# Moving every sixth softmax exponential of a two-layer transformer kernel from ScalarE to VectorE

## The chip, the cores and the metric

One core of one Trainium2 chip (trn2). The metric is the device time of one execution in microseconds (us). The kernel before takes 2283 us; most of its executions lie within 0.3% of each other. Engines are named as in the profile: PE is TensorE's matmuls, PEld its weight loads, ACT ScalarE, DVE VectorE, POOL GpSimd.

## The reference

Two layers, each an attention block and a feed-forward block with a residual, on 2048 rows of 512:

```python
def _A_ref(x, wqkv, wo):                      # S = 2048, D = 512
    H = 32; Dh = D // H                       # 32 heads of only 16
    qkv = transpose((x @ wqkv).reshape(B, S, 3, H, Dh), 2, 0, 3, 1, 4)
    scores = einsum("bhqd,bhkd->bhqk", q, k) * Dh ** -0.5
    p = softmax(scores)
    o = einsum("bhqk,bhkd->bhqd", p, v)
    return o.transpose(...).reshape(B, S, D) @ wo

def _B_ref(x, w1, w2):                        # F = 1792
    return silu(x @ w1) @ w2

x = x + _A_ref(layernorm(x), wqkv, wo)        # layer 0
x = x + _B_ref(layernorm(x), w1, w2)
x = x + _A_ref(layernorm(x), wqkv, wo)        # layer 1, the same weights
x = x + _B_ref(layernorm(x), w1, w2)
```

With heads of 16 the exponentials are many and the matmuls thin: 2 x 32 x 2048 x 2048 exponentials, in 4096 blocks of 128 keys by 512 queries.

## The kernel before

A "block" is one 128 x 512 piece of scores of one head. 64 blocks (16 key tiles of 4 heads) make a "group", whose result is one PSUM bank `o_ps` (a tile of 128 x 512 in fp32 is called a bank here). Blocks are taken three at a time. A step computes three scores, issues the P.V matmuls of the tile two steps back, and gives one exponential over 1536 columns to ACT:

```python
tiles = [blocks[i : i + NB] for i in range(0, len(blocks), NB)]      # NB = 3
...
for t, blks in enumerate(tiles):
    ...                                     # bg.ensure(...) of K, Q, V where needed
    s_ps = ps_s.tile([P, NB, 512], FP32, name="s_ps", tag="s")       # bufs=2: 6 PSUM banks
    for i, (L, qc, g, par, kt, j) in enumerate(blks):
        r = slice(32 * j, 32 * j + 32)
        nc.tensor.matmul(                   # scores: 32 rows of the array, 128 columns
            s_ps[:, i, :],
            lhsT=KT[L, kt // 4][r, g, (kt % 4) * P : (kt % 4 + 1) * P],
            rhs=QT[L, qc][r, g, par, :], start=True, stop=True)
    if t >= 2:
        emit_pv(t - 2)
    p_tiles[t] = ppool.tile([P, NB, 512], BF16, name="p_sb", tag="p")
    nc.scalar.activation(p_tiles[t][...], s_ps[...], ACT.Exp, scale=float(SCALE))
    if urgent:
        run_urgent()                        # transposes of a finished group
    else:
        bg.pump()                           # one piece of background work

def emit_pv(tile_i):
    for i, (L, qc, g, par, kt, j) in enumerate(tiles[tile_i]):
        ...
        nc.tensor.matmul(                   # P.V: 128 rows, 32 columns
            o_ps[32 * j : 32 * j + 32, :],
            lhsT=VA[L, kt // 4][:, kt % 4, 17 * h : 17 * h + 32],
            rhs=p_sb[:, i, :], start=(kt == 0), stop=(kt == NKT - 1))
        if kt == NKT - 1 and j == 3:        # group complete
            nc.vector.tensor_copy(out=oT[:], in_=o_ps[:])
            urgent.append(...)
```

All else (layer norms, Q, K, V and output projections, the feed-forward block) is "background": generators that `bg.pump()` advances by one piece a step. They share one PSUM bank (`ps_m`). Of the eight banks that the program uses six hold scores, one `o_ps`, one the background. The three score matmuls of a step use different 32-row strips of the array and run side by side (three within 0.61 us in the timeline below); so do the P.V matmuls in different 32-column strips.

The softmax here doesn't subtract the row's maximum and nothing guards it: scores larger than these inputs give would overflow.

## Time and profile before

| | before |
|---|---|
| time | 2283.2 us (median of 13) |
| exp on ACT | 1366 instructions, 1868 us busy |
| DVE busy | 414 us, 18% |
| PE busy | 1855 us, 81% |
| mean granted TensorE clock | 0.72 of full speed |

From the page of the kernel before. Busy time of the engines, then two of the rows that cut the span into 40 slices, in tenths (ACT busy, granted TensorE clock):

```profile
PE 1855.4 (81%) x10240; PEld 538.3 (24%) x10240; DVE 414.4 (18%) x746; ACT 1914.6 (84%) x1479; POOL 36.4 (2%) x47
...
ACT  1499989999999989999506999899989899999941
...
PEclk9995558985799767985666555799567965788556
```

ACT is full except at the start, at the layer boundary (slices 20 to 22) and in the tail. The clock is far from full in many slices.

The three costliest groups of the page (line, engine, operation, output<-inputs, shapes, count | busy us, mean ns of one | idle before them and its releaser):

```profile
L467 ACT ACTIVATE p_sb<-s_ps 128x1536 bf16<-128x1536 f32 x1366 | 1868.0, 1536 | 240.5 <-PE s_ps L456 239.5
L456 PE MATMUL s_ps<-QT,KT 32*128 32x512 bf16 x4096 | 705.3, 504 | 183.3 <-ACT p_sb L467 165.4
L399 PE MATMUL o_ps<-p_sb,VA 128*32 128x512 bf16 x4096 | 731.4, 513 | 42.0 <-DVE oT L408 41.8
```

A stretch of plain attention, no background work, in the windows view of the kernel before (busy us of each engine and number of instructions, then clock):

```profile
core 0: us, PE busy (x) PEld busy (x) DVE busy (x) ACT busy (x) POOL busy (x), PEclk, DMA share, GB/s
228.00:285.00 57.00, 48.90 (x257) 12.86 (x254) 2.75 (x6) 55.34 (x42) 0.00 (x0) 0.50 0.00 1
```

42 exponentials in 57 us, ACT 97% busy, and the clock exactly half. The timeline of the kernel before there (start, length, what):

```profile
227.56 6.98 ACT L467 ACTIVATE p_sb<-s_ps 128x1536 bf16<-128x1536 f32 x5
...
229.22 0.61 PE L456 MATMUL s_ps<-QT,KT 32*128 32x512 bf16 x3 [0.19 <-ACT p_sb L467]
...
229.77 0.61 PE L399 MATMUL o_ps<-p_sb,VA 128*32 128x512 bf16 x3
...
230.56 0.61 PE L456 MATMUL s_ps<-QT,KT 32*128 32x512 bf16 x3 [0.18 <-ACT p_sb L467]
```

One step takes 1.34 us. PE's two passes follow each other at 0.54 us and 0.80 us, of which 0.19 us is waiting for ACT: at half clock PE is nearly full too. In the same trace background matmuls of 512 columns, all of one shape, start 0.43 us apart at half clock and 0.23 at full (medians), so about 0.1 us of each 0.54 us comes on top. A pass of three matmuls side by side costs about 0.1 us more than one such background matmul at either clock (0.54 us against 0.43 at half, 0.32 against 0.23 at full); why, no run tested.

### The profile page before, as it was taken

How to read it: one execution, taken by the hardware profiler on the slowest of the kernel's cores; microseconds unless marked ns; L12 is line 12 of the kernel's file. 1: busy time of each engine (PE TensorE's matmuls, PEld its weight loads, DVE VectorE, ACT ScalarE, POOL GpSimd, SP SyncE). 2: the span in 40 equal slices, each digit the busy share in tenths (PEclk: the TensorE clock that was granted, in tenths of full speed). 3: DMA queues.
4: the chain of work that ended last, by engine and by line, in shares of the span. 5: the costliest groups of instructions: out<-in, count | busy, mean ns of one | idle time of the engine just before them, and what ended most of it. 6: DMA issues, size and time to landing. Idle time of an engine off the chain costs nothing.

```text
span 2282.7 us, 24321 instructions
## 1 busy us (share of the span) xinstructions
PE 1855.4 (81%) x10240; PEld 538.3 (24%) x10240; DVE 414.4 (18%) x746; ACT 1914.6 (84%) x1479; POOL 36.4 (2%) x47
## 2 busy tenths in 40 slices
PE   5788888888878888888667888878888888888866
PEld 1222222222222222222222222222222222222222
DVE  4430012120312112120221000311012100210021
ACT  1499989999999989999506999899989899999941
POOL 1100000000000000000000000000000000000000
PEclk9995558985799767985666555799567965788556
DMA  4000000000000000000000000000000000000000
GB/s 138 0 1 1 1 1 1 1 1 1 1 1 1 1 1 1 1 1 1 1 0 1 1 1 1 1 1 10 1 1 1 6 5 1 1 1 10 1 0 9
DMA packets 7917, 11.51 MB, mean 5 GB/s; under 512 B 384, under 2 KB 6784, under 8 KB 7808
## 3 DMA queue, kind: packets, MB, share of 16 engines
q1 hardware_dynamic: 7808, 9.96, 1.3%
q8 instruction: 80, 1.31, 0.2%
q14 instruction: 29, 0.24, 0.0%
HBM read 7.86 MB, written 2.10 MB: 4 GB/s over the span
## 4 chain that ended last, share of the span: by engine, by line
ACT 42%; PE 26%; issue 23%; DVE 9%; POOL 0%; DMA 0%; ACTq 0%; POOLq 0%; DVEq 0%
ACT p_sb L467 39%; PE s_ps L456 6%; PE o_ps L399 5%; PE h_ps L310 4%; ACT t_sb L320 3%; PE q_ps L214 2%; DVE QT L224 2%; PE f_ps L334 2%; PE v_ps L235 2%; PE k_ps L197 2%; DVE oT L408 2%; PE t_ps L177 1%; PE att L253 1%; DVE hT L321 1%; DVE st L152 1%
## 5 line engine op out<-in xcount | busy, mean ns | idle before, releaser
L467 ACT ACTIVATE p_sb<-s_ps 128x1536 bf16<-128x1536 f32 x1366 | 1868.0, 1536 | 240.5 <-PE s_ps L456 239.5
L456 PE MATMUL s_ps<-QT,KT 32*128 32x512 bf16 x4096 | 705.3, 504 | 183.3 <-ACT p_sb L467 165.4
L399 PE MATMUL o_ps<-p_sb,VA 128*32 128x512 bf16 x4096 | 731.4, 513 | 42.0 <-DVE oT L408 41.8
L456 PEld LDWEIGHTS <-KT 32*128 32x128 bf16 x4096 | 223.2, 95 | 726.5 <-issue 708.9
L399 PEld LDWEIGHTS <-VA 128*32 128x32 bf16 x4096 | 144.7, 98 | 500.2 <-issue 500.2
L310 PE MATMUL h_ps<-fT,w_sb 128*128 128x512 bf16 x448 | 169.1, 481 | 64.0 <-DVE hT L321 61.8
L408 DVE CAST oT<-o_ps 128x512 bf16<-128x512 f32 x64 | 44.1, 689 | 755.2 <-PE o_ps L399 754.8
L320 ACT ACTIVATE t_sb<-h_ps 128x512 f32<-128x512 f32 x112 | 73.5, 657 | 105.9 <-PE h_ps L310 105.9
L321 DVE SCALAR_TENSOR_TENSOR hT<-t_sb,h_ps 128x512 bf16<-128x512 f32 x112 | 77.0, 688 | 389.5 <-ACT t_sb L320 389.5
L334 PE MATMUL f_ps<-w_sb,hT 128*128 128x512 bf16 x448 | 129.5, 394 | 10.8 <-DVE hT L321 5.0
L310 PEld LDWEIGHTS <-w_sb 128*128 128x128 bf16 x448 | 39.4, 109 | 146.2 <-issue 142.2
L224 DVE TENSOR_SCALAR QT<-q_ps,mask 128x512 bf16<-128x512 f32 x64 | 45.1, 746 | 144.1 <-PE q_ps L214 144.1
L177 PE MATMUL t_ps<-ident,xn 128*128 128x128 bf16 x256 | 36.2, 308 | 38.6 <-DVE xn L163 33.1
L235 PE MATMUL v_ps<-w_qkv,xnT 128*128 128x512 bf16 x128 | 51.7, 531 | 18.5 <-DVE VA L244 12.7
L343 DVE SCALAR_TENSOR_TENSOR x_sb<-f_ps,x_sb 128x512 bf16<-128x512 f32 x32 | 22.1, 692 | 216.6 <-PE f_ps L334 216.6
L214 PE MATMUL q_ps<-xnT,w_qkv 128*128 128x512 bf16 x128 | 49.4, 478 | 14.1 <-DVE QT L224 13.1
L253 PE MATMUL att<-ident,oT 128*128 128x128 bf16 x256 | 35.0, 283 | 31.3 <-DVE hT L321 12.0
L197 PE MATMUL k_ps<-xnT,w_qkv 128*128 128x512 bf16 x128 | 47.1, 470 | 10.2 <-DVE xnT L182 3.9
L334 PEld LDWEIGHTS <-hT 128*128 128x128 bf16 x448 | 32.7, 99 | 67.9 <-issue 52.4
L289 PE MATMUL y_ps<-wo_sb,aT 128*128 128x512 bf16 x128 | 43.0, 428 | 4.6 <-DVE aT L283 1.6
L152 DVE BATCH_NORM_STATS2 st<-x_sb 128x6 f32<-128x512 bf16 x64 | 42.7, 667 | 3.0 <-DMA x_sb<-in_A_x_dram 3.0
L253 PEld LDWEIGHTS <-oT 128*128 128x128 bf16 x256 | 21.0, 121 | 88.8 <-issue 65.9
(30 smaller groups left out, 320.1 us busy)
## 6 DMA issues: line engine op xcount, KB each, us to landing
w_sb<-in_B_w_dram SPq DMA_DIRECT2D x2, 1792.0 KB, 14.1
x_sb<-in_A_x_dram SPq DMA_DIRECT2D x4, 512.0 KB, 8.8
out_dram<-x_sb SPq DMA_DIRECT2D x16, 128.0 KB, 1.7
w_qkv<-in_A_wqkv_dram SPq DMA_DIRECT2D x1, 1536.0 KB, 7.3
wo_sb<-in_A_wo_dram SPq DMA_DIRECT2D x1, 512.0 KB, 9.5
```

What stands on the lines that cost most here:

```text
L197: nc.tensor.matmul(k_ps[:], lhsT=w_qkv[:, ct, D + P * g : D + P * (g + 1)], rhs=xnT[L, c][:, ct, :], start=(ct == 0), stop=(ct == CT - 1),)
L214: nc.tensor.matmul(q_ps[:], lhsT=w_qkv[:, ct, P * g : P * (g + 1)], rhs=xnT[L, c][:, ct, :], start=(ct == 0), stop=(ct == CT - 1),)
L224: nc.vector.tensor_scalar_mul(out=QT[L, c][:, g, par, :], in0=q_ps[:], scalar1=masks[par][:, 0:1])
L235: nc.tensor.matmul(v_ps[:], lhsT=xnT[L, c][:, ct, tq * P : (tq + 1) * P], rhs=w_qkv[:, ct, 2 * D : 3 * D], start=(ct == 0), stop=(ct == CT ...
L310: nc.tensor.matmul(h_ps[:], lhsT=w1_sb[:, ct, ft * P : (ft + 1) * P], rhs=fT[:, ct, :], start=(ct == 0), stop=(ct == CT - 1),)
L320: nc.scalar.activation(t_sb[:], h_ps[:], ACT.Tanh, scale=0.5)
L321: nc.vector.scalar_tensor_tensor(out=hT[:, ft, :], in0=t_sb[:], scalar=1.0, in1=h_ps[:], op0=ALU.add, op1=ALU.mult,)
L334: nc.tensor.matmul(y_ps[:], lhsT=hT[:, ft, tq * P : (tq + 1) * P], rhs=w2_sb[:, ft, :], start=(ft == 0), stop=(ft == FT - 1),)
L399: nc.tensor.matmul(o_ps[32 * j : 32 * j + 32, :], lhsT=VA[L, kt // 4][:, kt % 4, 17 * h : 17 * h + 32], rhs=p_sb[:, i, :], start=(kt == 0) ...
L408: nc.vector.tensor_copy(out=oT[:], in_=o_ps[:])
L456: nc.tensor.matmul(s_ps[:, i, :], lhsT=KT[L, kt // 4][r, g, (kt % 4) * P : (kt % 4 + 1) * P], rhs=QT[L, qc][r, g, par, :], start=True, sto ...
L467: nc.scalar.activation(p_tiles[t][:, 0:n, :].rearrange("p a b -> p (a b)"), s_ps[:, 0:n, :].rearrange("p a b -> p (a b)"), ACT.Exp, scale= ...
```

## The change

The intent is to relieve ACT. ACT's tiles become 3 and 2 blocks in turn. At a rate of 0.6 a step one further block goes to DVE, which builds the exponential from bit operations: it scales the score into the bits of an fp16 number `y` whose exponent field is the integer part of the power of two, splits off the exponent (`e`) and the mantissa (`r`), and makes `r` into a cubic correction, so that exp = e + r up to a common factor. The sum `e + r` is not formed on DVE; both are multiplied by V, two P.V matmuls accumulating into the same `o_ps` strip. Besides, the transposes of a finished group are issued one step later (`due`), and the Q projections are spread, one group ahead, instead of in lumps.

```diff
-    NB = 3
+    D_RATE = 0.6
+    D_LAST = 52
-    ps_s = ...(name="ps_s", bufs=2, ...)
+    ps_s = ...(name="ps_s", bufs=1, ...)          # tags s3, s2, sd: 3 + 2 + 1 banks
@@ blocks into steps
+    while pos < len(blocks):
+        n = 3 - len(steps) % 2
+        a = blocks[pos : pos + n]; pos += n
+        d = []
+        credit = min(credit + D_RATE, 1.5)
+        if credit >= 1.0 and pos < len(blocks) and pos % 64 < D_LAST:
+            d = blocks[pos : pos + 1]; pos += 1; credit -= 1.0
+        steps.append((a, d))
@@ the exponential on DVE (emit_d, step_d; up to two blocks at a time)
+        nc.vector.tensor_scalar(out=pr["y"][:, len(pr["blks"]), :], in0=s_ps[:],
+            scalar1=float(1024 * SCALE * math.log2(math.e)),
+            scalar2=float(1024 * (15 - SHIFT)), op0=ALU.mult, op1=ALU.add)      # PSUM -> uint16
+            nc.vector.tensor_scalar(out=rf.bitcast(I32), in0=y.bitcast(I32),
+                scalar1=0x03FF03FF, scalar2=0x3C003C00, op0=ALU.bitwise_and, op1=ALU.bitwise_or)
+            nc.vector.tensor_scalar(out=ef.bitcast(I32), in0=y.bitcast(I32),
+                scalar1=0x7C007C00, scalar2=None, op0=ALU.bitwise_and)
+                nc.vector.tensor_tensor(out=rf, in0=rf, in1=rf, op=ALU.mult)
+                nc.vector.tensor_scalar(out=rf, in0=rf, scalar1=EXP_C, scalar2=EXP_A,
+                                        op0=ALU.mult, op1=ALU.add)
+                nc.vector.tensor_tensor(out=rf, in0=rf, in1=y.bitcast(FP16), op=ALU.mult)
@@ two P.V matmuls for each such block
+        for i, blk in enumerate(pr["blks"]):
+            pv(blk, [pr["e"][:, i, :].bitcast(FP16), pr["r"][:, i, :].bitcast(FP16)])
@@ main loop
+            due = bool(urgent)
...
-            if urgent:
+            if due:
                 run_urgent()
```

(Not shown: the pool sizes that make room, the bookkeeping of pairs and stages, and `next_q`, which queues one Q projection as each pair of groups begins.)

## The prediction

> **What bounds the kernel now.** In steady attention, the exponential on ACT: the page has ACT 84% busy, 1868 us in 1366 exp ACTIVATEs; the timeline at 228-236 us shows a three-block tile each 1.34 us; the windows view has ACT busy 55.3 of 57 us there. PE is close behind: the clock row reads 0.5 wherever no projection or FFN matmul runs, and a tile's score and P·V passes then take 0.54 us each, 1.08 of 1.34 us. At full clock they take 0.325 each. A pair of 128x512 background matmuls adds 0.54 us (full) or 0.97 (half). Of the 1366 tiles 733 have no background matmul, 599 of those at half clock. About 250 us at start, layer boundary (1110-1220 us) and tail are not limited by exp.
>
> **What the change does.** ACT tiles become alternately 3 and 2 blocks, still 1366 steps; 681 blocks (17%) get their exponential on DVE. ACT: 1.34 + about 0.91 us for two steps, 1.12 a step, about 290 us less. DVE: 681 evictions of 0.69 us (as the traced 128x512 casts), 470 us, plus 404 chains (277 of two blocks) of five SBUF operations. [...] DVE from 414 to about 1830 us, 80% busy and bursty. PE: each DVE block needs two P·V matmuls in one column group, which serialize: 2300 P·V passes instead of 1364, +0.29 us a step at half clock, +0.15 at full.
>
> **Net, by regime (us a step, before -> after).**
> - No background, half clock: 1.34 (ACT) -> 1.37 (PE).
> - No background, full clock: 1.34 -> 1.12.
> - Background every step, full clock: 1.34 -> 1.34 (PE).
> - FFN first half (three steps, four matmuls, a tanh): 4.7 -> 4.1 if the clock is full.
> - Background at half clock: 2.05 -> 2.34.
>
> So it hinges on the granted clock. [...] stretches show 0.5 or 1.0. Over its windows the clock rose where array fill (columns weighted by rows and columns used) passed about 0.34 of full-rate capacity and fell below about 0.31. Pure attention after, estimated: 0.25 at half clock, 0.31 at full, so it mostly stays at half. ACT's saving then turns into a wait for PE. Other terms: att transposes issued one step later save part of the 1.4 us lost at each of 64 group ends (-30 us); spread-out Q projections raise the clock more often (-30) but cost more at half (+20); evictions queue behind DVE chains (+50 to +100).
>
> This sum gives about 2250 us. The tuned-looking rate and cut-off constants make me think that clock or overlap comes out better, so I go lower: **2215 us, 8 in 10 within 2090 to 2340**. Chances: faster by over 2% 0.52, within 2% 0.30, slower by over 2% 0.18.
>
> **What would show it.** Exp group: 1366 ACTIVATEs, busy near 1580 us, idle grown, released by PE score matmuls. PE busy above 88%; DVE 75-90%. Clock still 0.5 in pure attention, 1.37 us a step; if it reads 1.0, 1.12 us and a time near 2050. Att steps under 2.8 us.
>
> **What would make it wrong.** A clock that stays full in attention (much faster); DVE operations slower than estimated, so that PE waits for DVE (slower); the clock failing to rise in FFN phases, the extra passes diluting the fill (slower).

## The result, and the profile after

| | before | after |
|---|---|---|
| time | 2283.2 us (13 runs) | 2219.9 us (8 runs, 2213.9 to 2225.8) |
| ratio of the fast runs | | 0.973 (0.971 to 0.974) |
| exp on ACT, busy | 1868 us | 1606 us |
| idle of ACT before them | 241 us | 416 us |
| DVE busy | 414 us | 1670 us |
| PE busy | 1855 us | 1796 us |
| mean granted clock | 0.72 | 0.88 |

A ratio here is the mean time of one kernel's fast runs over that of the other's in the same rounds, so it is not quite the ratio of the medians quoted beside it. All runs quoted are fast unless said.

The change saves 262 us of ACT's work, and 63 us of time. From the page of the changed kernel, the lines that answer to those above:

```profile
PE 1796.3 (81%) x10921; PEld 530.7 (24%) x10921; DVE 1670.1 (75%) x3447; ACT 1658.4 (75%) x1479; POOL 38.2 (2%) x47
...
ACT  1269998868888697878810998878898889788931
...
PEclk9899998988989888999856898889998998799966
```

PE did more matmuls (10921 against 10240) in less busy time, because the clock row is now 8 or 9 in most slices. No engine is full any more. The groups:

```profile
L591 ACT ACTIVATE p_sb<-s_ps 128x1536 bf16<-128x1536 f32 x1366 | 1606.2, 1260 | 415.5 <-PE d_ps L525 217.1
L525 PE MATMUL s_ps<-QT,KT 32*128 32x512 bf16 x3415 | 574.3, 413 | 109.0 <-ACT p_sb L591 106.7
...
L454 DVE TENSOR_SCALAR d_y<-d_ps 128x512 uint16<-128x512 f32 x681 | 467.1, 686 | 185.6 <-PE d_ps L525 184.2
...
L525 PE MATMUL d_ps<-QT,KT 32*128 32x512 bf16 x681 | 284.9, 418 | 54.9 <-DVE d_y L454 53.8
```

ACT's idle time has grown from 241 to 416 us, and ends with score matmuls: ACT waits for PE. The last line shows PE in turn waiting for DVE: the score of a DVE block needs the single bank `d_ps` back, and DVE's evictions stand in a queue behind its other operations. The same attention stretch, windows view of the changed kernel:

```profile
core 0: us, PE busy (x) PEld busy (x) DVE busy (x) ACT busy (x) POOL busy (x), PEclk, DMA share, GB/s
228.00:285.00 57.00, 45.99 (x324) 14.52 (x324) 50.23 (x107) 54.42 (x48) 0.00 (x0) 0.97 0.00 1
```

48 steps in place of 42, the clock 0.97 in place of 0.50, DVE at 88%. By the same view of the score tiles alone, 120 + 24 = 144 blocks were scored against 126: 396 ns a block against 452. Its timeline:

```profile
228.83 0.39 PE L525 MATMUL s_ps<-QT,KT 32*128 32x512 bf16 x2 [0.19 <-ACT p_sb L591]
...
230.17 0.39 PE L525 MATMUL s_ps<-QT,KT 32*128 32x512 bf16 x3 [0.63 <-ACT p_sb L591]
...
230.50 0.40 PE L424 MATMUL o_ps<-p_sb,VA 128*32 128x512 bf16 x3
230.51 0.60 PE L424 MATMUL o_ps<-d_e,VA 128*32 128x512 f16 x2
230.74 0.59 PE L424 MATMUL o_ps<-d_r,VA 128*32 128x512 f16 x2
...
231.25 0.39 PE L525 MATMUL s_ps<-QT,KT 32*128 32x512 bf16 x2
231.46 0.68 DVE L454 TENSOR_SCALAR d_y<-d_ps 128x512 uint16<-128x512 f32 x1
...
232.19 0.37 PE L525 MATMUL d_ps<-QT,KT 32*128 32x512 bf16 x1 [0.55 <-DVE d_y L454]
```

At 230.50 the P.V matmuls of a pair follow the tile's own: four more, of which the ones in one strip run one after the other (0.23 us from start to start). At 232.19 PE has waited 0.55 us for DVE, and with it all that is behind it in PE's queue.

**Where the 63 us came from.** The traces were cut into steps, from one step's first score matmul to the next's, and sorted by the background matmuls that PE ran in each. This table is worked out from the two traces; it is no view of the profile. "half" is the number of steps that began at clock 0.5. Steps are named after the PSUM tile of their background matmuls; those without any are called plain steps below. The last-but-one row takes together the attention output (a_ps, y_ps) and the K and V projections (k_ps, v_ps).

| background in the step | before: steps (half), mean us, sum | after: steps (half), mean us, sum | change |
|---|---|---|---|
| none | 733 (599), 1.30, 953 | 725 (97), 1.18, 853 | -100 us |
| att (end of a group) | 63 (34), 3.10, 195 | 63 (9), 1.98, 125 | -70 |
| q_ps | 59 (27), 1.78, 105 | 61 (0), 1.44, 88 | -17 |
| h_ps (FFN, first half) | 163 (41), 1.65, 270 | 166 (22), 1.77, 294 | +24 |
| f_ps (FFN, second half) | 154 (3), 1.34, 207 | 160 (5), 1.45, 231 | +24 |
| t_ps (layer norm) | 34 (34), 1.63, 55 | 32 (20), 2.40, 77 | +22 |
| a_ps, y_ps, k_ps, v_ps | 155, 1.38, 214 | 154, 1.70, 261 | +47 |
| start and layer boundary | 4, -, 158 | 4, -, 167 | +9 |

Plain attention, the group ends and the q_ps steps gain 187 us; the other steps with background work lose 117 us, with the start and the layer boundary 126 us in all. A row is not a phase, though. Measured from the first to the last h_ps matmul, group ends included, the FFN's first half got shorter (390 us before, 375 after, over the six of eight phases that lie within attention), although its own row says +24 us; the second half, from the first to the last f_ps matmul, did get longer (220 to 239 us). Experiment 1 says why the h_ps row misleads. The windows view shows the same over three slices full of background work, before and then after:

```profile
core 0: us, PE busy (x) PEld busy (x) DVE busy (x) ACT busy (x) POOL busy (x), PEclk, DMA share, GB/s
342.00:399.00 57.00, 48.15 (x306) 14.44 (x303) 15.87 (x31) 54.34 (x44) 1.27 (x2) 0.82 0.00 1
399.00:456.00 57.00, 47.33 (x288) 13.98 (x287) 8.25 (x13) 54.07 (x47) 0.00 (x0) 0.91 0.00 1
456.00:513.00 57.00, 50.65 (x317) 14.88 (x314) 15.85 (x29) 53.28 (x40) 3.19 (x3) 0.85 0.00 1
```

```profile
core 0: us, PE busy (x) PEld busy (x) DVE busy (x) ACT busy (x) POOL busy (x), PEclk, DMA share, GB/s
342.00:399.00 57.00, 47.56 (x293) 13.52 (x292) 45.13 (x95) 47.34 (x46) 1.61 (x2) 0.88 0.00 1
399.00:456.00 57.00, 51.23 (x319) 13.93 (x318) 43.70 (x92) 46.41 (x43) 0.00 (x0) 0.97 0.00 1
456.00:513.00 57.00, 47.71 (x279) 12.96 (x276) 45.86 (x96) 39.37 (x33) 3.19 (x3) 0.82 0.00 1
```

ACT falls from 162 to 133 us busy of 171; PE stays at 146.

### The profile page after: what moved, and what is told of

It reads as the page before. It is cut to its first block, busy times and chain, and to the rows that moved or that the text cites. A ratio compares the mean times of both kernels' runs of the same rounds, so it can differ in the third digit from the quotient of the medians.

```text
span 2221.2 us, 28337 instructions
## 1 busy us (share of the span) xinstructions
PE 1796.3 (81%) x10921; PEld 530.7 (24%) x10921; DVE 1670.1 (75%) x3447; ACT 1658.4 (75%) x1479; POOL 38.2 (2%) x47
## 4 chain that ended last, share of the span: by engine, by line
PE 37%; DVE 35%; ACT 18%; issue 9%; POOL 1%; DMA 0%; POOLq 0%; ACTq 0%; DVEq 0%
ACT p_sb L591 16%; PE o_ps L424 12%; DVE d_y L454 8%; PE s_ps L525 8%; PE f_ps L344 5%; PE h_ps L320 4%; DVE d_r L491 3%; DVE hT L331 3%; DVE d_r L473 3%; DVE d_r L492 3%; ACT t_sb L330 2%; DVE d_e L481 2%; DVE d_r L496 2%; PE v_ps L245 2%; DVE QT L234 2%
## 5 line engine op out<-in xcount | busy, mean ns | idle before, releaser
L591 ACT ACTIVATE p_sb<-s_ps 128x1536 bf16<-128x1536 f32 x1366 | 1606.2, 1260 | 415.5 <-PE d_ps L525 217.1
L454 DVE TENSOR_SCALAR d_y<-d_ps 128x512 uint16<-128x512 f32 x681 | 467.1, 686 | 185.6 <-PE d_ps L525 184.2
L525 PE MATMUL d_ps<-QT,KT 32*128 32x512 bf16 x681 | 284.9, 418 | 54.9 <-DVE d_y L454 53.8
L496 DVE TENSOR_TENSOR d_r<-d_r,d_y 128x1024 f16<-128x1024 f16 (+1 forms) x404 | 242.2, 599 | 2.8
L424 PE MATMUL o_ps<-d_r,VA 128*32 128x512 f16 x681 | 239.3, 412 | 5.0 <-DVE d_r L496 4.9
L491 DVE TENSOR_TENSOR d_r<-d_r 128x1024 f16<-128x1024 f16 (+1 forms) x404 | 241.9, 599 | 0.0
L424 PE MATMUL o_ps<-d_e,VA 128*32 128x512 f16 x681 | 241.0, 415 | 0.0
L492 DVE TENSOR_SCALAR d_r<-d_r 128x1024 f16<-128x1024 f16 (+1 forms) x404 | 161.5, 400 | 13.9
L473 DVE TENSOR_SCALAR d_r<-d_y 128x512 int32<-128x512 int32 (+1 forms) x404 | 155.0, 384 | 11.7
L481 DVE TENSOR_SCALAR d_e<-d_y 128x512 int32<-128x512 int32 (+1 forms) x404 | 152.6, 378 | 0.0
```

The lines of the kernel that those rows point to most:

```text
L424: nc.tensor.matmul(o_ps[32 * j : 32 * j + 32, :], lhsT=VA[L, kt // 4][:, kt % 4, 17 * h : 17 * h + 32], rhs=p, start=(o_count[key][j] == 0 ...
L454: nc.vector.tensor_scalar(out=pr["y"][:, len(pr["blks"]), :], in0=s_ps[:], scalar1=float(1024 * SCALE * math.log2(math.e)), scalar2=float( ...
L473: nc.vector.tensor_scalar(out=rf.bitcast(I32), in0=y.bitcast(I32), scalar1=0x03FF03FF, scalar2=0x3C003C00, op0=ALU.bitwise_and, op1=ALU.bi ...
L481: nc.vector.tensor_scalar(out=ef.bitcast(I32), in0=y.bitcast(I32), scalar1=0x7C007C00, scalar2=None, op0=ALU.bitwise_and,)
L491: nc.vector.tensor_tensor(out=rf, in0=rf, in1=rf, op=ALU.mult)
L492: nc.vector.tensor_scalar(out=rf, in0=rf, scalar1=EXP_C, scalar2=EXP_A, op0=ALU.mult, op1=ALU.add)
```

## The experiments

Two questions were open. Why did the clock rise in plain attention, which I had predicted not to happen? And which part of the change gains and which loses? Twelve kernels ran; "before" is their reference, near 2282 us.

### 1. The deferral alone (b_due) and its removal (a_nodue)

```diff
 # b_due: the kernel before
+            due = bool(urgent)
             s_ps = ps_s.tile(...)
-            if urgent:
+            if due:
                 run_urgent()
 # a_nodue: the changed kernel
-            if due:
+            if urgent:
```

> The kernel before with one line of the change alone: the transposes of a finished group are issued one step later, so that TensorE does not wait for the copy of o_ps. Nothing goes to VectorE. In the changed kernel the steps that hold the att transposes fell from 3.10 to 1.98 us on average, 63 of them, 70 us in all, as much as the whole gain of 63 us. Theory G (the deferral is worth a good part of that by itself, and the exponential on VectorE nets little): about 2235 us (2215 to 2250), att steps near 2.3 us, clock unchanged near 0.72. Rival H (those steps got shorter only because the steps themselves and the clock changed): 2270 us or more.

> The changed kernel without the deferral of the att transposes. Theory G: the 63 att steps grow by about 0.8 us each, 2270 us (2250 to 2290), which is the time before. Rival H: within 10 us of the changed kernel, 2220 us.

Measured: b_due 2273.5 us (0.996 of before, 0.994 to 0.998), a_nodue 2228.1 us (0.976). The deferral is worth 9 us in the one kernel and 8 in the other, against the 50 that theory G gave it. In a_nodue the att steps do take 2.80 us in place of 1.98, 52 us in all, but the steps around them take less (plain ones 825 us in place of 853, the h_ps ones 269 in place of 294). The stall had mostly been moved from the att step to its neighbours. The h_ps steps show it in the traces: those within three steps of an att step took 1.71 us before, 2.10 after and 1.76 in a_nodue (48 of them in each), those further away 1.63, 1.64 and 1.57. Theory G falls. It also warns about the table above: a wait saved in one class of steps can come back in another.

### 2. More PE work to lift the clock: repeated scores (b_warm)

```diff
 # the kernel before
+    for _ in range(2 if i == 0 and not bg.queue else 1):
         nc.tensor.matmul(s_ps[:, i, :], ...)      # the score, once more into the same place
```

> The kernel before, with the first score matmul of a tile issued twice (same operands, same result) in every step in which no background work is queued. It adds one serial pass to TensorE and no other work. Theory S (the clock follows the time in which any matmul streams: two passes in 1.343 us are 0.32 of the full-rate cycles, three are 0.48, and both traces together divide best near 0.42): attention runs at full clock, mean clock above 0.85, exp steps without background stay at 1.34 us because ScalarE bounds them, and background steps that stood at half clock speed up: about 2215 us (2200 to 2250). Rival F (my prediction's array fill, which is 0.23 here with the extra pass at half clock and 0.28 at full, under 0.31): the clock stays at 0.5 in attention, TensorE needs about 1.5 us a step and the time rises to 2350 us or more.

Measured: 2399.6 us (1.051), clock 0.70. The clock stayed down. The windows view of this run in plain attention:

```profile
228.00:285.00 57.00, 55.42 (x261) 9.02 (x260) 2.75 (x6) 51.68 (x37) 0.00 (x0) 0.50 0.00 1
```

PE is 97% busy, more than in the changed kernel (46 of 57 us), and is granted half clock. That is what theory F said, but not yet decisive against S: 37 tiles in 57 us make 1.54 us a step, in which three passes are 0.42 of the full-rate cycles, just at the threshold that S had assumed.

### 3. The twins: the same streaming time, rows or columns (b_sc2, b_pv2)

```diff
 # b_sc2: the kernel before
+    for _ in range(3 if i == 0 and not bg.queue else 1):
         nc.tensor.matmul(s_ps[:, i, :], ...)                       # 32 rows x 128 columns
 # b_pv2: the kernel before
+    for _ in range(2 if i == 0 and kt > 0 and not bg.queue else 0):
+        nc.tensor.matmul(o_ps[32 * j : 32 * j + 32, :], lhsT=zeros[:],   # 128 rows x 32 columns
+                         rhs=p_sb[:, i, :], start=False, stop=False)
```

> The kernel before, with the first score matmul of a tile issued three times (same result) in every step in which no background work is queued: two serial passes more of a matmul that uses 32 rows and 128 columns of the array. At half clock TensorE then needs about 0.54 + 0.54 + 2 x 0.43 = 1.93 us a step. Streaming time is then 0.44 of the full-rate cycles, array fill 0.22, active rows (each instant weighted by the share of the four 32-row groups in use) 0.25. Theory S (streaming time, threshold about 0.43): full clock, about 2215 us. Theory R (active rows, about 0.39 to rise and 0.37 to stay) and theory F (array fill, 0.34): the clock stays at half, 2640 us (2550 to 2700).

> The twin of the run with tripled score matmuls: the kernel before, with two matmuls of zero weights (adding exactly zero to the sums) ahead of the first P.V matmul of a tile in the same steps. Two serial passes of a matmul with 128 rows and 32 columns: the same streaming time 0.44 and the same fill 0.22 as its twin at half clock, but active rows 0.41. Theory R and theory S: attention goes to full clock and stays (active rows 0.60 there), exp steps stay at 1.34 us, background steps lose their half-clock share, about 2215 us (2190 to 2250), mean clock above 0.85. Theory F: half clock, 2640 us.

Measured: b_sc2 2659.5 us (1.165, from its fast runs; their mean clock is 0.68), b_pv2 2252.3 us (0.987, 0.985 to 0.989; mean clock 0.90). Both results are correct. The profile of b_sc2 fell in a slow execution (2709.5 us, mean clock 0.57, against 2654 to 2663 us and 0.68 in its fast runs); its times are not used, but its window shows that plain attention stays at half. b_sc2, then b_pv2:

```profile
228.00:285.00 57.00, 55.43 (x231) 11.26 (x231) 2.75 (x6) 39.72 (x28) 0.00 (x0) 0.50 0.00 1
```

```profile
228.00:285.00 57.00, 48.58 (x338) 15.96 (x337) 2.75 (x6) 56.34 (x42) 0.00 (x0) 0.97 0.00 1
```

Nearly the same number of extra passes (1234 in b_sc2, 1166 in b_pv2, which leaves out the first key tile of a group) of the same length (512 columns) and the same array fill gives half clock in one kernel and full clock in the other (0.50 and 0.97 in the windows above). What differs is the shape: 32 rows by 128 columns, or 128 rows by 32. So neither streaming time nor fill decides. A measure that fits is the share of the array's rows in use: each cycle is weighted by how many of the four 32-row strips a matmul streams through, transposes count in full, and the sum is taken as a share of full-rate cycles (a stretch at half clock counts half) over windows of 3.41 us. That is the shortest complete record of the clock in the traces of before and after; all other complete ones last whole multiples of it. The table counts the windows after which a single dividing line foretells the clock wrongly, with the best line for each measure. It was worked out twice from the traces (my first count put the lines for rows at 0.39 and 0.37); windows laid 0.05 or 0.15 us earlier change the counts, not the order.

| measure | before and after: rises (529), stays (726) | all 13 fast traces: rises (3536), stays (4738) |
|---|---|---|
| active rows | 20, 7 | 251, 104 (lines at 0.37 and 0.37) |
| time in which any matmul streams | 28, 17 | 563, 163 |
| array fill | 63, 44 | 575, 287 |

In the first two traces streaming time does almost as well as rows. The twins part them: in b_sc2's trace 323 of the 327 half-clock windows with streaming time of 0.42 or more were not followed by a rise, and their active rows were 0.25 (median). (That it is rows, and not something else in which these two shapes differ, is a reading of two shapes, not shown further.)

And so the kernel gains 1.3% (inside the 2% of "same", but clear of the noise) by multiplying with zeros: those matmuls lift the clock (0.90 in the mean, from 0.72), the exponentials stay at 1.34 us a step (42 in the window, as before), and the Q projections, group ends and some others, which used to stand at half clock, go faster.

### 4. The changed kernel without the second P.V matmul (a_e_only; wrong result)

```diff
-            pv(blk, [pr["e"][:, i, :].bitcast(FP16), pr["r"][:, i, :].bitcast(FP16)])
+            pv(blk, [pr["e"][:, i, :].bitcast(FP16)])
```

> Wrong result on purpose: the changed kernel with the second P.V matmul of each VectorE block (of d_r) left out; all VectorE work stays. P.V passes fall from 2300 to 1811. Theory P (background steps of the changed kernel are slowed by the extra P.V passes): the steps with background matmuls shorten by about 0.08 us at full clock and the time falls by 30 us or more, if the clock holds. Theory Q (they are slowed by PSUM evictions queued behind VectorE's chains): no gain there. Theory R on the clock: active rows at half clock fall to about 0.38, under the threshold, so that more of attention stands at half clock than in the changed kernel: mean clock 0.75 to 0.85 in place of 0.88, and the time 2200 to 2250 us all told.

Measured: 2275.4 us (0.997), clock 0.76. Removing 681 matmuls made the kernel 55 us slower. 437 of the 725 plain steps stand at half clock, against 97 in the changed kernel. Its window:

```profile
228.00:285.00 57.00, 52.53 (x271) 11.04 (x268) 45.09 (x95) 49.84 (x43) 0.00 (x0) 0.62 0.00 1
```

With the clock at 0.76 in the mean, the whole offload gains 0.3%. The time fell outside what I had expected (2200 to 2250 us): the loss of the clock weighed more than I had thought. The f_ps steps went from 231 to 223 us and the h_ps ones did not move, so theory P has some support here and not much.

### 5. The changed kernel with a shorter chain on DVE (a_short; wrong result)

```diff
-                nc.vector.tensor_tensor(out=rf, in0=rf, in1=rf, op=ALU.mult)
-                nc.vector.tensor_tensor(out=rf, in0=rf, in1=y.bitcast(FP16), op=ALU.mult)
```

> Wrong result on purpose: the changed kernel without the two tensor-tensor operations on d_r, which are 484 us of VectorE's 1670; TensorE's and ScalarE's work is untouched. Theory Q: the background steps fall back to their times of before (f 1.34, h 1.6, t 1.7, y 1.4 us), 80 to 120 us of the 126 us come back and the time is 2100 to 2140 us; attention without background, at 1.15 us, gains little. Theory P: 2190 us or more.

Measured: 2144.4 us (0.940): 75 us faster than the changed kernel for 436 us less of DVE's busy time (1234 in place of 1670 us), at about the same clock (0.90). So these two operations in DVE's queue do cost 75 us, though only half of it where I had looked. Plain steps gained 37 us (1.18 to 1.13), t_ps 14, att 9; f_ps, h_ps and k_ps steps gained 2, 0 and 3. The waits of PE for `d_ps`, in the waits view of the changed kernel and then of this one (us in total, times, longest):

```profile
PE d_ps L525 <- DVE d_y L454: 53.8, 60, 2.8
```

```profile
PE d_ps L522 <- DVE d_y L454: 30.3, 36, 1.5
```

The layer norm steps (t_ps), in which DVE is asked for both kinds of work, gained most per step (2.40 to 1.96 us, 1.63 before); in the FFN, where nothing was gained, DVE's queue is not the limit.

### 6. The changed kernel without the offload (a_d0)

```diff
-    D_RATE = 0.6
+    D_RATE = 0.0
```

> The changed kernel with no block sent to VectorE (rate 0): tiles of 3 and 2 blocks in turn, deferral and spread Q projections remain; 1639 steps instead of 1366. If VectorE's blocks are worth their cost (theory V): slower than the changed kernel, about 2300 us (2260 to 2340), and the clock back at half in attention because the serial passes are gone (two passes in about 1.12 us are 0.38). If the offload nets nothing (rival N): 2220 us or below.

Measured: 2417.4 us (1.060), clock 0.69. So, given its tiles of 3 and 2, the offload is worth 197 us. But those tiles, with the deferral and the spread Q projections, which this run keeps, cost 134 us against the kernel before: 1639 steps in place of 1366, and at half clock a plain step of 2.5 blocks takes 1.16 us, 0.46 us a block, where the kernel before needed 0.44 us. PE's two passes bound it, as its window shows (PE 97% busy at half clock):

```profile
228.00:285.00 57.00, 55.14 (x246) 12.53 (x244) 4.06 (x8) 53.36 (x48) 0.00 (x0) 0.50 0.00 1
```

The changed kernel had to earn this back first.

### 7. A version that offloads only in plain attention (a_mix, a_mixall; then a_mix2, a_mix2all)

In the FFN's second half PE sets the pace of the changed kernel. The timeline, PE only:

```profile
428.82 0.39 PE L525 MATMUL s_ps<-QT,KT 32*128 32x512 bf16 x3
428.83 0.39 PE L525 MATMUL d_ps<-QT,KT 32*128 32x512 bf16 x1
429.14 0.40 PE L424 MATMUL o_ps<-p_sb,VA 128*32 128x512 bf16 x3
429.48 0.60 PE L344 MATMUL f_ps<-w_sb,hT 128*128 128x512 bf16 x2
430.01 0.39 PE L525 MATMUL s_ps<-QT,KT 32*128 32x512 bf16 x2
```

PE has no gap; such a step takes 1.19 us with 2 blocks as with 3 (medians over the trace), and 1.62 us when it holds the extra P.V matmuls (50 of 160). Hence the idea to take three blocks on ACT in these steps and to use DVE only while no background work is queued. First with two score tiles of three banks, where in every second step the third bank may go to DVE (not shown: a pool for `d_e` of its own, and a rule that starts the chain of a single block after three steps; both are in all four versions):

```diff
+        use_d = odd and not bg.queue and (pos + 2) % 64 < D_LAST     # a_mixall: odd and True and ...
+        n = 2 if use_d else 3
-            s_ps = ps_s.tile([P, size, 512], FP32, name="s_ps", tag=f"s{size}")
+            s_ps = ps_s.tile([P, 3, 512], FP32, name="s_ps", tag=f"s{t % 2}")
-                emit_d(blk)
+                emit_d(blk, s_ps[:, 2, :])
```

> A version built on what the runs showed. Both score tiles have three PSUM banks, as in the kernel before. In every second step the third block goes to VectorE, but only while no background work is queued; in all other steps ScalarE takes all three. 235 blocks go to VectorE in place of 681. Theory P (background steps of the changed kernel are bound by TensorE, whose steps cost as much with 2 blocks as with 3, plus the extra P.V passes): background steps return to about the times of before (f 1.34, h 1.6 us) while attention without background keeps 1.12 us and full clock: 2150 us (2110 to 2200). Rival (each block given to VectorE earns its share wherever it runs, so that fewer of them cost time): slower than the changed kernel, 2240 us or more.

> The control of the run before: the same tiles, but the third block goes to VectorE in every second step whether or not background work is queued (554 blocks). It has the structure of the version before it and nearly the offload of the changed kernel. Theory P: background steps are slowed again by the extra passes, 2200 us (2170 to 2230), slower than its twin by 30 us or more. Rival: faster than its twin.

Measured: a_mix 2257.7 us (0.989), a_mixall 2365.8 us (1.035). Both missed by far. The waits view of a_mixall says why:

```profile
ACT p_sb L592 <- DVE d_y L450: 358.5, 397, 18.5
```

ACT's exponential of two blocks waited for DVE's eviction of the third, since both read one tile; the wait went away when they no longer did (below). In a_mix this wait is 90 us (112 times), so there it is only part of the miss. Plain steps took 1.37 and 1.40 us. The order between the twins was as theory P said, but under another limit. So the third block got a bank of its own, and ACT takes it in an ACTIVATE of 512 columns where DVE does not:

```diff
+            if n > size:                                   # the third block of an odd step, on ACT
+                x_ps = ps_s.tile([P, 512], FP32, name="x_ps", tag="sd")
+                score(a_blks[2], x_ps[:])
...
+            if n > size:
+                nc.scalar.activation(p_tiles[t][:, 2, :], x_ps[:], ACT.Exp, scale=float(SCALE))
```

> In the last two runs the shared PSUM tile made ScalarE wait for VectorE's eviction (358 us in the control), which hid what they were made for. Here the third block of every second step has a bank of its own: VectorE takes it while no background work is queued, and otherwise ScalarE does, in a second ACTIVATE of 512 columns. 235 blocks go to VectorE. Theory P (extra P.V passes are worth it only where TensorE has time to spare): steps without background near 1.2 us, background steps as in the version with the shared tile (f 1.37, y 1.36, k 1.5, v 1.3 us): 2140 us (2100 to 2190), faster than the changed kernel. Rival (every offloaded block earns its share): slower than the changed kernel.

> The control: the same, but VectorE takes the third block of every second step whether or not background work is queued (554 blocks). Theory P: slower than its twin by 30 us or more, near the changed kernel, 2200 us (2170 to 2230). Rival: faster than its twin.

Measured: a_mix2 2202.0 us (0.966, 0.962 to 0.969), a_mix2all 2220.3 us (0.974, 0.973 to 0.975). The wait of ACT for `d_y` is gone from both waits views. a_mix2 sends 235 blocks to DVE where the changed kernel sends 681, and is faster than both kernels, by 3.4% and about 0.8% (the changed kernel was timed in other rounds; their ratios to the kernel before, 0.962 to 0.969 and 0.971 to 0.974, do not overlap); the twin with 554 blocks only equals the changed kernel. So theory P holds in direction: taken together, the blocks offloaded in steps with background work cost more than they bring. It was too large in size: 18 us between the twins, not 30 or more, and 2202 us in place of 2140. By classes of steps a_mix2 gains on its twin in t_ps (59 against 80 us), y_ps, q_ps, k_ps and f_ps (7 to 11 each), and loses in h_ps (295 against 275), where ACT also has the tanh (whether that is why, no run tested), and in plain steps (905 against 890), 294 of which stand at half clock against 213.

## Why the prediction was right or wrong

The time, the range and the sign were right: 2215 us predicted, 2219.9 measured. The argument behind them was not, so that the close hit was luck. The sum gave 2250 us and I took 35 us off on a hunch; two terms of the sum were wrong by more than that, in opposite directions.

- **"Pure attention ... mostly stays at half. ACT's saving then turns into a wait for PE": this step failed.** 628 of 725 plain steps ran at full clock, and took 1.15 us there, where 1.12 had been predicted for full clock. The cause is the step before it, "array fill (columns weighted by rows and columns used)". In the trace of before alone, fill misjudges only 11 of 377 windows for a rise and 3 of 257 for a stay, and active rows 7 and 2: both fit, probably because nearly everything that raised the clock there was 128 by 128. The new P.V matmuls, 128 rows by 32 columns, tell them apart. The very passes that I counted only as PE's cost also lifted its clock (a_e_only: 55 us slower without the second one; b_pv2: about 30 us faster with useless ones).
- **"If it reads 1.0, ... a time near 2050" failed as well**: the clock read 0.97 in that stretch and 0.88 in the mean. "Background every step, full clock: 1.34 -> 1.34" measured 1.45 for f_ps, and the FFN's first half, "4.7 -> 4.1" for three steps, went from 4.61 to 4.43 us (the six phases within attention, first to last h_ps matmul, 84 such triples). Background steps other than att and q_ps lost 117 us, with the start and the layer boundary 126.
- **"evictions queue behind DVE chains (+50 to +100)"**: right in size as far as tested, 75 us by a_short, which takes out two of the five chain operations; but half of it fell in plain attention.
- **The deferral, "-30 us"**: -8 to -9 us.
- **Spread Q projections**: not tested by themselves. The q_ps steps took 105 us before, 105 in a_e_only and 88 after, which goes with the clock.
- **DVE's costs were right**, though what a chain would take was my estimate, shown by no trace then. A pair's five operations take 683 + 683 + 448 + 427 + 420 ns in the mean, 2.66 us: 1024 fp16 elements take 448 ns in a tensor_scalar (427 in the median) and 683 in a tensor_tensor. Busy time came to 1670 us and not 1830, since operations overlap their neighbours in the trace: their durations add up to 1839 us.
- **ACT's costs were right**: 1366 exponentials, 1606 us busy against 1580. PE busy came to 81%, not above 88%: the clock again.

The clock records of before and after (68 and 108) read 0.5 or 1.0 and nothing between, and the activity of the window before foretells most of them: by active rows 27 of 1255 windows are misjudged. The clock did not follow PE's busy share: 55.4 of 57 us busy at half clock in b_warm, 48.6 at 0.97 in b_pv2.

The h_ps steps, 1.65 us before and 1.77 after, moved neither with shorter DVE chains nor with fewer P.V matmuls (1.77 in both). They did move with the deferral: 1.62 in a_nodue. Of their 24 us, 19 lie within three steps of a group end (experiment 1). So most of this loss is the stall of the group ends, booked elsewhere. What stays open is why the f_ps steps near group ends took 1.59 us in place of 1.34 (1.38 further away), with the deferral or without it.

## What to carry to other kernels

Before costing an offload, ask what the extra matmuls do to TensorE's clock: here the share of rows in use fitted best, a thin matmul over all 128 rows lifted the clock (0.90 in the mean, b_pv2) and one over 32 rows did not (0.68, b_sc2), and with its second P.V matmul, which lifts the clock, the offload gained 2.7%, without it 0.3%. A threshold fitted to one trace is only as good as the shapes in that trace; a pair of kernels that differ in one shape is a cheap test of it. And when three engines are all near 80%, place the moved work by phase: 235 blocks moved in plain attention alone beat 554 moved everywhere by 18 us in the same structure.

## Further figures of this case

- Two extra passes a step of 32 rows x 128 columns left the mean clock at 0.68 (2659 us), and two of 128 rows x 32 columns gave 0.90 (2252 us). In the fit, active rows of about 0.37 of the full-rate cycles in a window divided half from full, with 355 of 8274 windows misjudged in 13 traces.
- In the fit of active rows over the traces of before and after, counting transposes in full misjudged 20 rises and 7 stays, with half weight 25 and 11, not at all 27 and 25. This is a fit, no run of transposes alone.
- Bitwise operations on 512 int32 elements took 420 to 427 ns in SBUF, near the 448 ns (median 427) of a tensor_scalar on the same bytes as 1024 fp16 elements; 256 took 286 to 290 ns, against 294 for 512 of fp16.
- Exponentials without a wait between them, with their input in PSUM, started 1.33 us apart for 1536 columns and 0.90 us for 1024 in the trace of after: 0.83 ns a column and about 52 ns.
